# A spectral mixer with an MLP on one core: when the gates' row is multiplied in, and in which order w1's and w2's rows are loaded

## The chip, the cores and the metric

The kernel runs on one core of one Trainium2 chip. The metric is the device time of one execution in microseconds (us). Seven resources of the core matter here: PE (TensorE, the matmuls), DVE (VectorE), ACT (ScalarE), POOL (GpSimd), SP (SyncE, which only issues DMA transfers), the 16 DMA engines, and PSUM, the banks that matmuls write and that DVE and ACT read. Each engine carries out its own instructions strictly in order and waits at an instruction until the work that it needs has been done.

## The reference

```python
def _A_ref(x, ...):                      # Fourier mixing
    a = einsum("bsd,ed->bse", x, dft_hid_re); b = einsum("bsd,ed->bse", x, dft_hid_im)
    return einsum("ts,bse->bte", dft_seq_re, a) - einsum("ts,bse->bte", dft_seq_im, b)
def _B_ref(x, w1, b1, w2, b2):           # the MLP
    h = gelu(einsum("bsd,df->bsf", layernorm(x), w1) + b1)
    return einsum("bsf,fd->bsd", h, w2) + b2
x = A_x                                  # 1 x 2048 x 1024
sa, ca, ga, sb, cb, gb = six rows of silu(c) @ w_mod
x = x + ga * _A_ref(layernorm(x) * (1 + ca) + sa, ...)
x = x + gb * _B_ref(layernorm(x) * (1 + cb) + sb, w1, b1, w2, b2)
```

The inner size of the MLP is 3584, all numbers are float32. `gb` is the row of gates: 1024 numbers, one per column, the same for each of the 2048 tokens.

## The kernel before

**Number format.** The float32 operands are split into a high and a low part in float16, and each product takes three passes (high x high, high x low, low x high). ACT makes the high part (L2379), DVE the low part (L2391). The big products follow Strassen's idea: 7 products of half-size blocks instead of 8, in the order 0, 1, 2, 4, 3, 6, 5. The sums of blocks that this needs are called combs here; DVE adds them (L2405). All data lies in one tensor of the on-chip memory, so nearly every tile has the name `arena`; `ps` is PSUM, `fw` are split weights that were stored in DRAM and are loaded again.

**Stages.** First the two Fourier products and the residual. Then, for 16 tiles of 128 tokens in 8 blocks b0 to b7, the second layer norm: sums (L3138, L3139), squares on ACT (L3120), a root (L2620 on ACT, L2626 on DVE, twice per block), scalings (L3158, L3162 on DVE, L3171 on ACT), a store of the residual to the output (L3148, on SP's queue), eight transposes on PE (L3181: "turn" 0 to 15, one for each tile; 12 and 13 belong to b6, 14 and 15 to b7), copies out of PSUM (L3185), and the split of the result into parts that go to DRAM (L3211, L3220, L3233, stores L3226). Beside it PE computes the six rows of `w_mod` (L2900; loads L2894, a copy out of PSUM by ACT L2923; DVE multiplies `b2` by the gates at L2928, POOL stores the rows at L2924 and L2929).

Then the MLP: `gemm3(g)`, g = 0 to 27, computes the first product (L3628, 7 products of 12 matmuls), each g for 128 columns of w1 and their partners, and `gemm4(v)`, v = 0 to 13, the second (L3742, 2 token blocks of 7 products of 12 matmuls). A half of the tokens is done at v = 0 to 6, the other at v = 7 to 13. The first two g are interleaved (`gemm3_first`): their first products are products 1, 2, 3, 4 and so on in the text, and products 1 to 3 start at 312.04, 318.23 and 322.07 us, product 4 at 341.75. For these, ACT copies a PSUM bank out (L3928), DVE adds the next product to it (L3933) and ACT takes the gelu (L3924); later g use L3650, L3654 and L3647. Results of `gemm4` go to eight running sums `acc`: ACT writes the first ones (L3782), DVE adds all others (L3792). Some products of `gemm4` add onto a bank that already holds another product, and so can start only when that one has been read.

**The loads of weights.** w1 is split once for each g below 14, w2 once for each v below 7. For the first g the split parts were stored early and are loaded again (L3480 for g 0 and 1, L3487 for g 2). Raw rows of w1 for g 3 and 4 are loaded at L3491 (four loads of 256 KB), and at L3494 four loads of 512 KB bring rows of w2 whose sum of squares sets the scale `s2c` of w2's split for v = 0 (L3311 on ACT squares them, L3319 on DVE and L3323 on POOL add them up). The rows for the split itself come at L3497.

**What sets the order.** The program is written by a list planner that runs when the kernel is built. Work is pushed as tasks in streams, each with an engine, a cost, the tasks that it depends on and a due time. The planner keeps a modelled clock for each engine and, whenever PE's next product is placed, puts in front of it those tasks of the other engines that can run by then, those with the earlier due time first. A load is a task of SP's queue in the same way. So a due time doesn't delay anything on the chip: it changes the order in which instructions stand on each engine, and through the modelled clocks that of all that follow.

**The gates.** After `gemm4(5)` and `gemm4(12)`, the last but one of each half, `gb_tasks` multiplies the eight sums `acc` by the row of gates (L3830, 128 x 1024 each); the last `gemm4` of the half then adds its products scaled by the same row. In the second half four further additions (L3835) bring in rows of the output that were stored before (loads L3823), since the last stores don't add.

## Time and profile before

| | |
|---|---|
| time, median of 3 runs | 1378.37 us (1377.45 to 1378.69) |
| profiled execution | 1377.23 us, span 1375.4 us |
| mean granted clock of PE | 0.972 |
| PE busy | 1291.3 us, 94% of the span, 6081 matmuls |
| DVE busy | 1088.4 us, 79% |
| ACT busy | 746.6 us, 54% |
| POOL busy | 265.1 us, 19% |
| L3628, first product | 2352 matmuls, 515.5 us |
| L3742, second product | 2352 matmuls, 513.2 us |
| HBM traffic | 222 GB/s over the span |

The span is that of the profiled execution from its first instruction to its last. The profile's rows name an engine, a line of the kernel, an operation and its tiles (output, arrow, inputs), how many instructions a row joins, and in square brackets the idle time just ahead of it on that engine and what ended it. A row of the timeline begins with its start and its duration in us. "SPq" is an instruction of SP's that issues a DMA transfer; such rows show when it was issued, not when the data had landed.

### The profile page before, as it was taken

What the parts mean: (1) busy time and instruction counts of PE and PEld (TensorE: products, weight loads), DVE (VectorE), ACT (ScalarE), POOL (GpSimd) and SP (SyncE); (2) the same over time, 40 slices, a digit from 0 to 9 for tenths busy, and PEclk for the clock granted to TensorE, in tenths of its full rate; (3) what the DMA queues carried; (4) which work ended last, traced back from release to release, by engine and by line L of the source; (5) the groups of instructions that cost most, each with busy time, mean ns of one, the idle gap of its engine ahead of it and who ended that gap; (6) DMA issues with size and microseconds to landing.
All of it is one profiled execution on the core that took longest, in us unless ns stands there. A gap on an engine that the chain in (4) does not pass through costs nothing.

```text
span 1375.4 us, 17329 instructions
## 1 busy us (share of the span) xinstructions
PE 1291.3 (94%) x6081; PEld 622.9 (45%) x6081; DVE 1088.4 (79%) x1623; ACT 746.6 (54%) x1188; POOL 265.1 (19%) x426
## 2 busy tenths in 40 slices
PE   5888899777989999999999999999999999999997
PEld 1445466543434444444444444444444444444443
DVE  5888789998588999898989996566685858687695
ACT  4476557877667747474746433256545353636330
POOL 2000010102102000000000000254553433553201
PEclk9888899998999999999999999999999999999999
DMA  9777046569536957575453555999797878786524
GB/s 368 307 250 231 1 169 169 133 194 381 218 145 200 320 146 226 171 204 187 153 184 130 200 205 223 262 349 338 252 318 240 296 264 294 268 306 235 176 81 111
DMA packets 109754, 306.22 MB, mean 223 GB/s; under 512 B 14076, under 2 KB 14076, under 8 KB 107736
## 3 DMA queue, kind: packets, MB, share of 16 engines
q1 hardware_dynamic: 76776, 197.73, 40.5%
q0 software_dynamic: 32880, 107.29, 25.9%
q8 instruction: 49, 0.80, 0.2%
q14 instruction: 49, 0.40, 0.1%
HBM read 220.03 MB, written 84.93 MB: 222 GB/s over the span
## 4 chain that ended last, share of the span: by engine, by line
PE 67%; DVE 9%; ACT 4%; issue 2%; DMA 2%; SPq 0%; POOL 0%; DVEq 0%; ACTq 0%; POOLq 0%
PE ps L3742 34%; PE ps L3628 32%; ACT arena L2379 1%; DVE arena L2391 1%; DVE arena L3220 1%; DVE arena L2405 1%; DVE arena L3162 1%; PE ps L3046 1%; DVE arena L3233 1%; DMA arena<-fw 1%; DMA fzc<-arena 1%; ACT arena L3211 1%; DVE arena L3792 0%; DMA arena<-in_w_dram 0%; PE ps L3058 0%
## 5 line engine op out<-in xcount | busy, mean ns | idle before, releaser
L3628 PE MATMUL ps<-arena 128*128 128x512 f16 x2352 | 515.5, 381 | 9.4 <-DMA arena<-fw 4.8
L3742 PE MATMUL ps<-arena 128*128 128x512 f16 x2352 | 513.2, 380 | 8.0 <-ACT arena L3782 6.2
L3628 PEld LDWEIGHTS <-arena 128*128 128x128 f16 x2352 | 230.8, 98 | 289.9 <-issue 10.8
L3742 PEld LDWEIGHTS <-arena 128*128 128x128 f16 x2352 | 230.7, 98 | 288.3 <-issue 12.0
L3792 DVE SCALAR_TENSOR_TENSOR arena<-ps,i4c,arena 128x1024 f32<-128x1024 f32 x179 | 229.5, 1282 | 104.9 <-PE ps L3742 100.4
L2379 ACT ACTIVATE arena<-arena,shc 128x512 f16<-128x512 f32 (+1 forms) x115 | 115.8, 1017 | 137.2 <-DVE arena L2405 80.3
L2391 DVE SCALAR_TENSOR_TENSOR arena<-arena,shc 128x512 f16<-128x512 f32 (+1 forms) x115 | 129.0, 1121 | 29.6 <-ACT arena L2379 29.2
L2405 DVE TENSOR_TENSOR arena<-arena 128x512 f32<-128x512 f32 (+1 forms) x196 | 148.5, 764 | 3.7
L3533 ACT ACTIVATE arena<-arena 128x512 f32<-128x512 f32 (+5 forms) x148 | 91.2, 617 | 108.8 <-DVE arena L3542 84.8
L3647 ACT ACTIVATE arena<-arena,b1s,i1c 128x512 f32<-128x512 f32 x78 | 63.4, 813 | 90.0 <-DVE arena L3654 88.1
L2379 ACT ACTIVATE arena<-arena,s1c 128x512 f16<-128x512 f32 (+1 forms) x70 | 60.9, 886 | 66.5 <-DVE arena L2405 42.2
L3654 DVE TENSOR_TENSOR arena<-arena,ps 128x512 f32<-128x512 f32 x78 | 53.4, 685 | 52.4 <-PE ps L3628 51.7
L3542 DVE TENSOR_TENSOR arena<-arena 128x256 f32<-128x256 f32 x240 | 87.9, 421 | 1.7 <-DMA arena<-in_cre_dram 1.7
L3323 POOL PARTITION_ALL_REDUCE sums<-sums x21 | 10.4, 501 | 405.0 <-DVE sums L3319 405.0
L3559 POOL DMA_DIRECT2D arena<-in_cim_dram x99 | 54.5, 551 | 92.3 <-ACT arena L3533 86.1
L2391 DVE SCALAR_TENSOR_TENSOR arena<-arena,s1c 128x512 f16<-128x512 f32 (+1 forms) x70 | 65.8, 958 | 5.0 <-ACT arena L2379 4.9
L3559 POOL DMA_DIRECT2D arena<-in_cre_dram x99 | 54.6, 552 | 68.3 <-ACT arena L3533 50.9
L3650 ACT ACTIVATE arena<-ps 128x512 f32<-128x512 f32 x78 | 45.8, 588 | 35.8 <-PE ps L3628 35.6
L2391 DVE SCALAR_TENSOR_TENSOR arena<-arena,s2c 128x1024 f16<-128x1024 f32 x49 | 62.0, 1279 | 0.9 <-ACT arena L2379 0.9
L3046 PE MATMUL ps<-arena 128*128 128x256 f16 (+3 forms) x400 | 51.7, 290 | 10.1 <-DVE arena L3073 10.1
L2900 PE MATMUL ps<-arena,scol 128*128 128x512 f32 x128 | 58.3, 602 | 0.3 <-ACT arena L2915 0.3
L2379 ACT ACTIVATE arena<-arena,s2c 128x1024 f16<-128x1024 f32 x49 | 55.0, 1137 | 5.8 <-DVE arena L2405 5.8
(204 smaller groups left out, 1230.7 us busy)
## 6 DMA issues: line engine op xcount, KB each, us to landing
fw<-arena SPq DMA_DIRECT2D x71, 512.0 KB, 5.0
arena<-fw SPq DMA_DIRECT2D x119, 256.0 KB, 4.9
arena<-fw SPq DMA_DIRECT2D x49, 512.0 KB, 7.0
arena<-in_cre_dram POOLq DMA_DIRECT2D x96, 256.0 KB
arena<-in_cim_dram POOLq DMA_DIRECT2D x96, 256.0 KB
arena<-in_wm_dram SPq DMA_DIRECT2D x32, 512.0 KB, 7.5
arena<-in_w_dram SPq DMA_DIRECT2D x32, 512.0 KB, 6.4
arena<-in_w_dram SPq DMA_DIRECT2D x56, 256.0 KB, 4.5
```

The source lines that it names most:

```text
L2379: act.activation(o[m][0], q(j), AF.Copy, **sc)
L2391: dve.scalar_tensor_tensor(o[m][1], q(j), scale, o[m][0], op0=ALU.mult, op1=ALU.subtract)
L2405: dve.tensor_tensor(q(d), q(a), q(b), op=op)
L2900: pe.matmul(bank((6 if n < 3 else 4) + h), scol[:, k : k + 1].to_broadcast([P, P]), FA(o + 512 * h, (1, 512)), start=k == 0, stop=k == 7,)
L3046: pe.matmul(PA(pb + o, (1, w)), l, r, start=n == 0, stop=n == len(mm_) - 1)
L3533: f = lambda: act.activation(sq(a), sq(a), AF.Square, accum_out=csum[0:pn, n : n + 1])
L3542: dve.tensor_tensor(a[:, o::2], a[:, o::2], b[:, o::2], op=op)
L3559: return lambda t: gp.dma_start(t[0:pn], v)
L3628: pe.matmul(ps.rearrange("p (k t) -> p k t", k=4), w1c[:, m, s, a, d * P : (d + 1) * P], zc(m)[:, b, :, d, :], start=(start and d == 0 and ...
L3647: act.activation(dst, src, AF.Gelu_apprx_tanh, scale=inv, bias=b1s[:, 2 * p + j : 2 * p + j + 1])
L3742: pe.matmul(t[:, j], hidc[:, c_, m, a, k * P : (k + 1) * P], w2c[:, m, c_, w], start=(start and c_ == 0 and n == 0), stop=(c_ == 1 and n = ...
L3792: lambda: dve.scalar_tensor_tensor(dst, ps[b], inv, dst, op0=ALU.mult, op1=ALU.add), kp[b],
```

## The change

Two edits. First, the four loads at L3494 (w2's rows for the squares of v = 0) get the due time 300 in place of 240; the four loads of w1's rows just above have 250. Second, the eight multiplications by the gates are pushed in two lots of four: those of token block 0 already within `gemm4(5)` and `gemm4(12)`, at the third product of token block 1, each now depending on the last product of its own block; those of block 1 after `gemm4` as before, with the four additions.

```diff
     for q in range(4):
         f = lambda q=q: sp.dma_start(early2(q), w2[0:2, :, q, :].rearrange("j p x -> p j x"))
-        load(("early2", q), f, [("P", 15), ("Q", 15)], 1.5, "rw3", 240.0)
+        load(("early2", q), f, [("P", 15), ("Q", 15)], 1.5, "rw3", 300.0)
...
-    def gb_tasks(h):
+    def gb_tasks(h, blk):
+
 
         t = []
-        for i in range(8):
+        for i in range(4 * blk, 4 * blk + 4):
             f = lambda i=i: dve.tensor_tensor(acc_tile(i), acc_tile(i), gb2_t, op=ALU.mult)
-            t.append(Task("dve", 1.23, f))
-        if h:
+            t.append(Task("dve", 1.23, f, [("acc", blk, 5)]))
+        if h and blk:
             for m, (r, hf) in LASTQ.items():
...
             if v == NV - 1 or blk == 0:
                 return
+            if v in (5, 12) and slot == 2:
+                push("gb", "gb", gb_tasks(v // 7, 0), due[4, v + 1] - 25.0)
...
             if v in (5, 12):
-                push("gb", "gb", gb_tasks(v // 7), due[4, v + 1] - 25.0)
+                push("gb", "gb", gb_tasks(v // 7, 1), due[4, v + 1] - 25.0)
```

No instruction of PE, DVE or ACT is added or removed by these edits, but the planner's order changes between about 300 and 640 us on every engine but PE, and at the two places of the multiplications. On PE only transposes move. Three places matter below; names and lines of a row are those above, with three lines more from `gb_tasks` on (old L3830 is L3831, L3835 is L3836, L3924 is L3927, L3928 is L3931, L3933 is L3936).

The first is SP's queue from the loads of w2 on, around 300 to 330 us. Before:

```order
L3494 DMA arena_65<-in_w_dram 128x2x512 x3
L3491 DMA arena_65<-in_w_dram 128x512 x2
L3148 DMA out_dram<-arena_65 128x1024
L3491 DMA arena_65<-in_w_dram 128x512 x2
L3487 DMA arena_65<-fw_2_78 128x1024
L3480 DMA arena_65<-fw_0_76 128x1024
L2894 DMA arena_65<-in_wm_dram 128x1024 x5
L3480 DMA arena_65<-fw_1_77 128x1024
L3148 DMA out_dram<-arena_65 128x1024
L2926 DMA arena_65<-in_b_dram 128x1024
```

After:

```order
L3491 DMA arena_65<-in_w_dram 128x512 x2
L3494 DMA arena_65<-in_w_dram 128x2x512 x3
L3148 DMA out_dram<-arena_65 128x1024
L3494 DMA arena_65<-in_w_dram 128x2x512
L3487 DMA arena_65<-fw_2_78 128x1024
L3148 DMA out_dram<-arena_65 128x1024
L3480 DMA arena_65<-fw_0_76 128x1024
L2894 DMA arena_65<-in_wm_dram 128x1024 x5
L3480 DMA arena_65<-fw_1_77 128x1024
L3480 DMA arena_65<-fw_0_76 128x1024
L3480 DMA arena_65<-fw_1_77 128x1024
L2926 DMA arena_65<-in_b_dram 128x1024
```

The second store L3148 (b7's first tile) has moved from behind the first reloads L3480 and the five loads of `w_mod` to ahead of them, and two reloads more stand ahead of the load of `b2` (L2926).

The second is ACT around 335 to 350 us, where the last block b7 (`lns_22`) is normalised. Before:

```order
L2923 ACTIVATE arena_65<-ps 128x1024
L3185 ACTIVATE arena_65<-ps 128x1024
L3211 ACTIVATE arena_65<-arena_65 128x2x512
L3120 ACTIVATE arena_65,lns_22_142<-arena_65,lns_22_142 128x1024
L3185 ACTIVATE arena_65<-ps 128x1024
L3120 ACTIVATE arena_65,lns_22_142<-arena_65,lns_22_142 128x1024
L3928 ACTIVATE arena_65<-ps 128x512
L2620 ACTIVATE lns_22_142<-lns_22_142,eps_13_114 128x2
```

After:

```order
L3120 ACTIVATE arena_65,lns_22_142<-arena_65,lns_22_142 128x1024 x2
L3311 ACTIVATE arena_65,sums_2282<-arena_65 128x1024
L3211 ACTIVATE arena_65<-arena_65 128x2x512
L3311 ACTIVATE arena_65,sums_2282<-arena_65 128x1024
L3211 ACTIVATE arena_65<-arena_65 128x512
L2923 ACTIVATE arena_65<-ps 128x1024
L3185 ACTIVATE arena_65<-ps 128x1024
L2620 ACTIVATE lns_22_142<-lns_22_142,eps_13_114 128x2
L2621 ACTIVATE lns_22_142<-lns_22_142,eps_13_114 128x2
L3931 ACTIVATE arena_65<-ps 128x512
```

The root L2620 of b7 stood behind the copy of product 4 (L3928) and now stands ahead of it (L3931); its squares L3120 stand ahead of L2923.

The third is DVE around 1328 to 1345 us, between `gemm4(12)` and `gemm4(13)`. Before:

```order
L3830 TENSOR_TENSOR arena_65<-arena_65 128x1024
L2405 TENSOR_TENSOR arena_65<-arena_65 128x512 x2
L3792 SCALAR_TENSOR_TENSOR arena_65<-ps,i4c_152,arena_65 128x2x512
L3835 TENSOR_TENSOR arena_65<-arena_65 128x2x512
L3792 SCALAR_TENSOR_TENSOR arena_65<-ps,i4c_152,arena_65 128x2x512
L2405 TENSOR_TENSOR arena_65<-arena_65 128x512
L2391 SCALAR_TENSOR_TENSOR arena_65<-arena_65,shc_149 128x512
L3835 TENSOR_TENSOR arena_65<-arena_65 128x2x512 x2
```

After:

```order
L2391 SCALAR_TENSOR_TENSOR arena_65<-arena_65,shc_149 128x512 x2
L2405 TENSOR_TENSOR arena_65<-arena_65 128x512 x3
L3792 SCALAR_TENSOR_TENSOR arena_65<-ps,i4c_152,arena_65 128x2x512
L2391 SCALAR_TENSOR_TENSOR arena_65<-arena_65,shc_149 128x512 x2
L3792 SCALAR_TENSOR_TENSOR arena_65<-ps,i4c_152,arena_65 128x2x512
L2391 SCALAR_TENSOR_TENSOR arena_65<-arena_65,shc_149 128x512
L2405 TENSOR_TENSOR arena_65<-arena_65 128x512
L3836 TENSOR_TENSOR arena_65<-arena_65 128x2x512 x2
```

No multiplication stands any more directly ahead of the combs L2405 of the last g, and the additions (L3835, now L3836) stand behind them.

## The prediction

> **What bounds the kernel now.** I read the page first, then what PE (TensorE) waits for, PE's timeline, the two 20-us windows in which it is slow, and last the rows of the engines that it waits for there.
>
> ```profile
> PE 1291.3 (94%) x6081; PEld 622.9 (45%) x6081; DVE 1088.4 (79%) x1623; ACT 746.6 (54%) x1188; POOL 265.1 (19%) x426
> ```
>
> ```profile
> PE ps L3742 <- ACT arena L3782: 6.2, 1, 6.2
> PE ps L3628 <- DMA arena<-fw: 4.8, 2, 3.7
> PE ps L3628 <- DVE arena L3073: 3.3, 1, 3.3
> PE ps L3742 <- DVE arena L3792: 1.4, 2, 1.2
> PE ps L3628 <- ACT arena L3650: 1.3, 2, 0.7
> PE ps L3742 <- DVE arena L2391: 0.4, 1, 0.4
> ```
>
> The first line is the page's: PE is busy in 94% of the span, and its number of matmuls doesn't change. The six others are every wait of the MLP's products (L3628 first, L3742 second product; columns: us in total, times, longest). PE's timeline says where they lie:
>
> ```profile
> 312.04 5.28 PE L3628 MATMUL ps<-arena 128*128 128x512 f16 x12 [3.29 <-DVE arena L3073]
> ...
> 322.07 2.76 PE L3628 MATMUL ps<-arena 128*128 128x512 f16 x12 [1.09 <-DMA arena<-fw]
> ...
> 341.75 17.25 PE L3628 MATMUL ps<-arena 128*128 128x512 f16 x72 [3.73 <-DMA arena<-fw]
> ...
> 368.54 1.09 PE L3181 MATMUL ps<-ident,arena 128*128 128x128 f32 x8 [0.90 <-ACT arena L3185]
> 369.47 23.65 PE L3628 MATMUL ps<-arena 128*128 128x512 f16 x108
> 392.95 5.34 PE L3742 MATMUL ps<-arena 128*128 128x512 f16 x24
> 404.50 33.82 PE L3742 MATMUL ps<-arena 128*128 128x512 f16 x144 [6.21 <-ACT arena L3782]
> ...
> 476.21 4.05 PE L3742 MATMUL ps<-arena 128*128 128x512 f16 x18
> ...
> 1339.71 1.04 PE L3742 MATMUL ps<-arena 128*128 128x512 f16 x4 [0.43 <-DVE arena L2391]
> ...
> 1344.89 22.18 PE L3742 MATMUL ps<-arena 128*128 128x512 f16 x102 [1.25 <-DVE arena L3792]
> ```
>
> So the waits lie in two places: the hand-over from the transforms to the MLP (312 to 476 us) and 1339 to 1345 us. Between 476 and 1339 the products never wait. What PE gains or loses before 476 therefore reaches the end unchanged, and DVE work moved between those times is worth nothing unless it makes PE wait. The early multiplications at v=5 (about 800 us) lie there: I cost them at nothing; their cover is PE's unbroken work.
>
> A matmul costs 23.65/108 = 0.219 us at full clock. After the wait of 6.21 the 144 took 33.82 instead of 144 x 0.219 = 31.5: 2.3 us for a lower clock. After the wait of 3.73 the 72 took 1.5 more than 15.8. In the windows of 20 us that hold the waits of 3.29 and 6.21 (the last three columns are the granted clock, the DMA share and GB/s) the granted clock is 0.83, so the loss is the clock's:
>
> ```profile
> 310.00:330.00 20.00, 16.48 (x61) 7.72 (x61) 16.74 (x32) 16.66 (x28) 4.20 (x7) 0.83 1.02 397
> 390.00:410.00 20.00, 13.79 (x53) 5.62 (x52) 18.68 (x19) 11.73 (x14) 1.41 (x2) 0.83 0.50 191
> ```
>
> The Trainium skill (TensorE: Matmul & The Clock Gate, "What's actually happening") says that after an idle window of about 3.4 us the array runs at half clock until it has been busy for about as long. By that the penalty would be about 1.7 us, an estimate from the page; the sum would then come out 0.6 us smaller. The row's 2.3 decides here.
>
> **The loads.** The change puts 4 loads of 512 KB of w2 behind w1's 4 of 256 KB. The bytes are the same, and in both orders all eight stand ahead of the reload (L3480) that product 3 waits for, so this alone moves nothing. What matters is what the planner then did: on SP the store L3148 of b7's first tile (b7 is the last token block) now stands ahead of that reload (old issue 317.78) instead of behind it.
>
> ```profile
> 317.78 0.38 SPq L3480 DMA_DIRECT2D arena<-fw  x1
> ...
> 328.49 0.34 SPq L3148 DMA_DIRECT2D out_dram<-arena  x1
> ...
> 332.44 4.29 SPq L3480 DMA_DIRECT2D arena<-fw  x4
> ```
>
> ```profile
> SPq L3148 <- DVE arena L3139: 6.5, 1, 6.5
> ```
>
> ```profile
> fw<-arena SPq DMA_DIRECT2D x71, 512.0 KB, 5.0
> arena<-fw SPq DMA_DIRECT2D x119, 256.0 KB, 4.9
> ```
>
> In the old order that store blocked SP for 6.5 us, because its sum L3139 came late on DVE. In the new order L3139 follows its first half L3138 at once, both ahead of the L3158 pair:
>
> ```profile
> 313.64 2.48 DVE L3158 SCALAR_TENSOR_TENSOR arena<-arena,lns 128x1024 f32<-128x1024 f32 x2
> 316.03 1.22 DVE L3138 TENSOR_TENSOR arena<-arena 128x1024 f32<-128x1024 f32 x1
> ...
> 327.24 1.22 DVE L3139 SCALAR_TENSOR_TENSOR arena<-arena 128x1024 f32<-128x1024 f32 x1
> ...
> 348.74 0.69 DVE L3933 TENSOR_TENSOR arena<-arena,ps 128x512 f32<-128x512 f32 x1 [6.29 <-PE ps L3628]
> ```
>
> So it ends at 313.64 + 2 x 1.22 = 316.1, and SP, which reaches the store at 317.8, hardly waits. Product 3's reload has one more transfer of 512 KB ahead, 1.3 us at the window's 397 GB/s, and one issue (0.34): **product 3 +1.7**, at 323.8, ending at 326.6. Bounds: 0 (hidden among transfers in flight) and +12 (the store stays at 328.49: the second rival).
>
> Product 3's copy on ACT now stands ahead of b6's second squares (L3120):
>
> ```profile
> 323.48 1.13 ACT L3120 ACTIVATE arena<-arena,lns 128x1024 f32<-128x1024 f32 x1
> ...
> 334.93 1.02 ACT L2923 ACTIVATE arena<-ps 128x1024 f32<-128x1024 f32 x1 [0.95 <-PE ps L2900]
> ...
> 346.08 0.60 ACT L3928 ACTIVATE arena<-ps 128x512 f32<-128x512 f32 x1 [4.95 <-PE ps L3628]
> 346.58 0.29 ACT L2620 ACTIVATE lns<-lns,eps 128x2 f32<-128x2 f32 x1
> ...
> 356.94 1.23 ACT L3171 ACTIVATE arena<-arena,lns 128x1024 f32<-128x1024 f32 x1
> ```
>
> They start at 326.6 + 0.6 = 327.2 instead of 323.48, so turn 12, the w_mod rows L2900 behind it and L2923 come **3.7 later** (L2923 at 338.6). Product 4's reload (old issue 332.44) takes a buffer that those L2900 rows free, and stands behind the store of b7's second tile, whose L3139 comes on DVE after b6's root: 327.2 + two squares 2.3 + roots and small ones 1.4 + 0.7 + 2 x 1.22 = 334.0. With two loads between it is issued near 336.0. The old one took 9.3 us to product 4's start, behind five w_mod loads; these are now 1.7 later and this one 3.5, so I take the mean of the page, 4.9: **product 4 at 340.9** (old 341.75). The ends are 4.9 and 9.3, so up to 345.3.
>
> **The last token block.** b7's root L2620 no longer stands behind product 4's copy, which waited 4.95 us for PE. It comes after L2923 and one more copy of the same length: 338.6 + 2 x 1.02 = 340.6, **6.0 us earlier**. From the old root to L3171 were 10.4 us, of which 2.3 went by on DVE behind L3933 (348.74) and 1.6 on ACT behind a copy. L3171 comes between 340.6 + 6.5 = 347.1 and 351.0, instead of 356.94. PE reaches turn 14 after 12 matmuls, turn 13 and 36 matmuls: 340.9 + 48 x 0.219 + 1.1 = 352.5, so nothing waits there. After 48 more comes turn 15 at 364.0 (old 368.54), after 120 more the second product: 364.0 + 1.0 + 26.3 = 391.3, against 392.95: **-1.6**. (12 matmuls more than before stand behind turn 15, which takes 2.6 of the 4.5 back.) One step is later: the row store of the gates (L2929) has its multiplication L2928 behind an add of product 6 now, near 351; with 5.0 for a store it lands at 357, and the copy that waits for it is asked for by PE at 353.5 + 24 x 0.219 = 358.8. Hidden by 1.2; bounds 0 and +2.
>
> **The wait of 6.21.** The third product of gemm4(0) adds onto a bank that ACT must have read:
>
> ```profile
> 400.23 3.23 ACT L2379 ACTIVATE arena<-arena,s2c 128x1024 f16<-128x1024 f32 x3 [3.10 <-DVE arena L2405]
> 403.36 1.09 ACT L3782 ACTIVATE arena<-ps,i4c 128x1024 f32<-128x1024 f32 x1
> ```
>
> The read (L3782) stands behind splits of w2, and these behind combs on DVE. In the new order two of five splits stand earlier, and splits of w1 (L2391) behind. Between DVE's last add of the first pair and the last comb I count 10 L2391 (8 x 1.28, 2 half as wide x 0.64), 9 L2405 (4 x 1.22, 5 x 0.71) and 3 L3654 (0.68), by the rows below: 22 us. The add follows the first 12 matmuls behind turn 15: 365.0 + 2.6 + 0.7 = 368.3. The last comb ends at 390.3, with 2 us for waits on ACT at 392.3; two splits of 1.08 and L3782 end at 395.6. PE asks at 391.3 + 5.3 = 396.6. **-6.2**, and with it the lower clock **-2.3**. Bounds: all stays (0) or all goes (-8.5); I take all, and each us over the margin of 1.0 would cost one.
>
> **The next hand-over, gemm4(1).** What is late next: five of the seven low splits of w2 (L2391) and two combs now stand behind the last add of the g before, all ahead of the first L3792. In the old order one did.
>
> ```profile
> 464.10 1.22 DVE L2405 TENSOR_TENSOR arena<-arena 128x1024 f32<-128x1024 f32 x1
> ...
> 474.02 0.68 DVE L3654 TENSOR_TENSOR arena<-arena,ps 128x512 f32<-128x512 f32 x1
> 474.62 1.28 DVE L2391 SCALAR_TENSOR_TENSOR arena<-arena,s2c 128x1024 f16<-128x1024 f32 x1
> ```
>
> The add ends 1.5 us before PE starts gemm4(1) (474.70, 476.21). Then 5 x 1.28 + 2 x 1.22 + 1.28 for L3792 = 10.1, so the eviction is in 8.6 us after PE's start; the third product asks at 5.3: **+3.3**. Bounds: 0 (the splits run earlier than their place) and +5.6 (with a clock penalty of 2.3).
>
> **The end.** At v=12 two of the sixteen multiplications go between evictions of the same round, and hid27's combs (L2405) stand directly ahead of gemm4(13)'s first L3792, the kept adds behind:
>
> ```profile
> 1330.52 1.41 DVE L2405 TENSOR_TENSOR arena<-arena 128x512 f32<-128x512 f32 x2
> ```
>
> The waits of PE at 1339 to 1345 (0.43, 1.25 and the 0.15 that makes the row's 1.4) end on DVE. With two multiplications (2.4 us) and two adds out of the way they go: **-1.8**; bounds 0 and -1.8. On SP the four loads of kept rows now follow w2's seven loads; their adds stand later too, beside PE's last 102 matmuls (22.18 us), so I cost that at nothing; if they came later than that, the end would move.
>
> **Sum.** -1.6 - 6.2 - 2.3 + 3.3 - 1.8 = -8.6 us. The profiled execution took 1377.23 us (span 1375.4), 1.1 below the runs' median of 1378.37; the sum goes to the median: **1369.8**, or -0.6%. Covered work: w2's scale comes later with its squares (L3311 on ACT), but they stand ahead of L2923 (338.6), and their first user, the split of w2 (L2379), stands behind turn 15's copies.
>
> **Rivals.**
> 1. The third product still waits. DVE is busy 18.68 of 20 us in the window 390 to 410; if its work, not the transposes, sets the end of this stage, the 8.5 stay, and with them the old lead of DVE at gemm4(1), so the 3.3 falls away: -1.6 - 1.8, 1375.0.
> 2. Slower: the store L3148 on SP waits until its old 328.49. Product 3's reload, five w_mod loads and product 4's reload stand behind it, and PE idles 12 us more. As the forecast has PE without a wait from 340.9 on, each us late there reaches the end: -8.6 + 12 = +3.4, with 2.3 more for the clock, 1381.8 to 1384.1. It decides from 8.6 us late. For it: that store did wait 6.5. Against: L3138 ran at 316.03 with no wait.
> 3. The stage doesn't change in sum (b6's 3.7 late and product 4's slower reload eat b7's gain); only the end does: 1376.6.
>
> **Chances.** Forecast 0.55, rival 1 0.13, rival 3 0.10, rival 2 and anything slower 0.17, better than 1363 0.05. The forecast's own range is 1364 (without the 3.3 and with the 0.9 and 1.3 of old waits gone too: -14.1) to 1374 (product 4 at 345.3: +4.4). The range that takes in rivals 1 and 3 is 1363 to 1379. A difference under 0.2% (2.8 us) can't be told from none: forecast, better and half of rival 1 make faster 0.68 (half of rival 1 is 0.07, rounded up), the rest of it and rival 3 same 0.15, slower 0.17.
>
> **What will show it.** Right: SP's wait on L3139 ahead of product 3 gone, b7's root near 341, turn 14 near 352 and turn 15 near 364 without a wait, the row of 144 matmuls starting near 397 at about 31.5 us, gemm4(1) starting 8 to 11 us before 476 with a wait of some 3 us at its third product, and the rows of 1339 to 1345 gone. Wrong: an SP wait ahead of product 3 that stays, product 4 later than 346, a wait of L3742 on L3782 that stays, or new waits of PE between 476 and 1339.

## The result, and the profile after

| | before | after |
|---|---|---|
| median of the runs side by side | 1377.45 us (1375.72 to 1378.69) | 1371.72 us (1370.14 to 1374.18) |
| ratio | | 0.9964, 95% interval 0.9947 to 0.9981 |
| profiled execution | 1377.23 us, span 1375.4 | 1370.87 us, span 1368.9 |
| mean granted clock | 0.972 | 0.974 |

The changed kernel is 5.7 us (0.4%) faster; 8.6 us were forecast. The profiled executions differ by 6.5 us in the span, and the rows up to the experiments are read from these two. PE's timeline of the changed kernel, in the same place as the one shown for before:

```profile
324.24 4.45 PE L3628 MATMUL ps<-arena 128*128 128x512 f16 x12 [3.34 <-DMA arena<-fw]
...
343.78 2.76 PE L3628 MATMUL ps<-arena 128*128 128x512 f16 x12 [1.53 <-DMA arena<-fw]
...
355.41 1.09 PE L3181 MATMUL ps<-ident,arena 128*128 128x128 f32 x8 [0.21 <-ACT arena L3171]
356.34 5.34 PE L3628 MATMUL ps<-arena 128*128 128x512 f16 x24
363.61 5.34 PE L3628 MATMUL ps<-arena 128*128 128x512 f16 x24 [1.93 <-ACT arena L3931]
368.78 1.04 PE L3181 MATMUL ps<-ident,arena 128*128 128x128 f32 x8
...
395.56 5.34 PE L3742 MATMUL ps<-arena 128*128 128x512 f16 x24
401.18 31.24 PE L3742 MATMUL ps<-arena 128*128 128x512 f16 x144 [0.29 <-ACT arena L3782]
432.26 36.42 PE L3628 MATMUL ps<-arena 128*128 128x512 f16 x168
468.52 5.34 PE L3742 MATMUL ps<-arena 128*128 128x512 f16 x24
476.62 31.25 PE L3742 MATMUL ps<-arena 128*128 128x512 f16 x144 [2.75 <-DVE arena L3792]
507.71 12.46 PE L3628 MATMUL ps<-arena 128*128 128x512 f16 x57
...
1305.42 18.29 PE L3628 MATMUL ps<-arena 128*128 128x512 f16 x84
...
1335.74 24.77 PE L3742 MATMUL ps<-arena 128*128 128x512 f16 x114 [0.37 <-DVE arena L3792]
```

The reader is to see four things. The wait of 6.21 us is now 0.29, and the 144 matmuls behind it take 31.24 us instead of 33.82. Yet gemm4(0) starts at 395.56, later than before (392.95). A wait of 2.75 has come to gemm4(1). And of the waits that before has between 1339 and 1345 us one of 0.37 is left (at 1335.74 here).

For the bookkeeping, PE's rows of before that the prediction did not need, from the end of gemm4(0) to the end of gemm4(1):

```profile
438.16 5.34 PE L3628 MATMUL ps<-arena 128*128 128x512 f16 x24
...
476.21 36.42 PE L3742 MATMUL ps<-arena 128*128 128x512 f16 x168
512.47 0.81 PE L3628 MATMUL ps<-arena 128*128 128x512 f16 x3
```

The forecast's sum against the two timelines (after less before, us):

| term | forecast | measured | from |
|---|---|---|---|
| start of gemm4(0) | -1.6 | +2.6 | 395.56 - 392.95 |
| wait of its third product | -6.2 | -5.9 | 0.29 - 6.21 |
| clock behind it | -2.3 | -2.6 | 31.24 - 33.82 |
| g behind it: the two waits on L3650 (1.3) and 0.5 around them, at full clock (1.00) | none | -1.8 | 438.16 to 476.21 is 38.05, 432.26 to 468.52 is 36.26 |
| gemm4(1) | +3.3 | +2.9 | 468.52 to 507.71 is 39.19, 476.21 to 512.47 is 36.26 |
| end | -1.8 | -1.8 | from the start of the row of 84 L3628 to the end of the last L3742: 55.09, before 56.88 |
| sum | -8.6 | -6.6 | span -6.5 |

Between the first product behind gemm4(1) and the row of 84 L3628 the changed kernel takes 797.71 us (1305.42 - 507.71) and before 797.72 (1310.19, where that row starts in its timeline, - 512.47). So the multiplications at v = 5 moved nothing that PE shows, as forecast.

One correction to the description of the kernel: products 1 to 7 are all of g 0 and those of g 1 follow, so product 3 is the third of g 0. No step of the prediction rested on it.

### Where the start of gemm4(0) was lost

The one term with the wrong sign begins at product 3. SP's queue (issues), then what SP waited for between 305 and 322 us and between 330 and 340 us:

```profile
317.13 0.34 SPq L3487 DMA_DIRECT2D arena<-fw  x1
317.56 0.38 SPq L3148 DMA_DIRECT2D out_dram<-arena  x1
318.03 0.38 SPq L3480 DMA_DIRECT2D arena<-fw  x1
...
336.12 0.34 SPq L3148 DMA_DIRECT2D out_dram<-arena  x1
...
337.87 1.29 SPq L3480 DMA_DIRECT2D arena<-fw  x2
```

```profile
SPq L3487 <- PE ps L3628: 5.6, 1, 5.6
```

```profile
SPq L3148 <- DVE lns L3150: 5.5, 1, 5.5
```

From 305 to 322 us SP also waited 5.2 us for DVE's L3139; that is for the store before, issued at 310.52, which waited 5.9 us for DVE in the kernel before too. The store of b7's first tile (317.56) issues right behind L3487, which waited for product 1 to end; DVE's sum had ended at 315.9 and didn't hold it. So the second rival's mechanism did not come: the reload was issued at 318.03, only 0.25 us after before's 317.78. But its data arrived later: from issue to product 3 it was 6.2 us, before 4.3. That is the +1.7 that was forecast for one more transfer of 512 KB, with 0.2 on top. What the forecast left out is that PE's wait there grew from 1.09 to 3.34 us, and that product 3 then ran at a low clock: 4.45 us instead of 2.76 (granted clock 0.60 from 324.3 to 328.6 us, in before 1.00 from 322.1 to 324.8).

The delay passes on. ACT, DVE and POOL of the changed kernel:

```profile
329.22 1.14 ACT L3120 ACTIVATE arena<-arena,lns 128x1024 f32<-128x1024 f32 x1
...
344.11 0.30 ACT L2620 ACTIVATE lns<-lns,eps 128x2 f32<-128x2 f32 x1
...
362.96 0.60 ACT L3931 ACTIVATE arena<-ps 128x512 f32<-128x512 f32 x1 [2.51 <-DMA frow_gbb<-arena]
...
396.92 3.21 ACT L2379 ACTIVATE arena<-arena,s2c 128x1024 f16<-128x1024 f32 x3
400.04 1.09 ACT L3782 ACTIVATE arena<-ps,i4c 128x1024 f32<-128x1024 f32 x1
```

```profile
346.01 0.15 DVE L3327 TENSOR_SCALAR sums<-sums 128x1 f32<-128x1 f32 x1 [1.84 <-POOL sums L3323]
...
346.91 0.16 DVE L2626 RECIPROCAL lns<-lns 128x2 f32<-128x2 f32 x1
...
354.59 1.22 DVE L2928 TENSOR_TENSOR arena<-arena 128x1024 f32<-128x1024 f32 x1
...
471.69 3.67 DVE L2391 SCALAR_TENSOR_TENSOR arena<-arena,s2c 128x1024 f16<-128x1024 f32 x3
475.28 2.66 DVE L3792 SCALAR_TENSOR_TENSOR arena<-ps,i4c,arena 128x1024 f32<-128x1024 f32 x2
```

```profile
356.11 0.56 POOL L2929 DMA_DIRECT2D frow_gbb<-arena  x1 [2.85 <-DVE arena L2928]
```

b6's second squares start at 329.22 (forecast 327.2), the store of b7's second tile is issued at 336.12 (its sum was forecast for 334.0), product 4's reload at 337.87 (336.0) and product 4 at 343.78 (340.9). Then the row of gates: L2928 runs at 354.59 (near 351), its store L2929 lands when ACT goes on at 362.96, 6.9 us after its issue, and PE waits 1.93 us at 363.61. On DVE the scale of w2 (L3327 and what follows) waits 1.84 us for POOL and stands ahead of b7's root (L2626), which had been ready since 344.4.

The last two rows of ACT show why the wait of 6.21 is gone: ahead of the three splits of w2 and L3782 ACT had stood idle for 3.10 us before, for a comb of DVE's, and now it starts them at 396.92 without a wait.

### The profile page after: what moved, and what is told of

It is laid out like the page before. It is cut to its first block, busy times and chain, and to the rows that moved or that the text cites. A ratio compares the mean times of both kernels' runs of the same rounds, so it can differ in the third digit from the quotient of the medians.

```text
span 1368.9 us, 17332 instructions
## 1 busy us (share of the span) xinstructions
PE 1290.3 (94%) x6081; PEld 623.7 (46%) x6081; DVE 1089.1 (80%) x1623; ACT 747.7 (55%) x1188; POOL 263.8 (19%) x426
## 4 chain that ended last, share of the span: by engine, by line
PE 67%; DVE 10%; DMA 2%; ACT 2%; issue 2%; SPq 1%; POOL 0%; DVEq 0%; POOLq 0%; ACTq 0%
PE ps L3742 34%; PE ps L3628 32%; DVE arena L2391 2%; DVE arena L3220 1%; DVE arena L3162 1%; DVE arena L2405 1%; DVE arena L3233 1%; ACT arena L2379 1%; PE ps L3046 1%; DMA arena<-in_wm_dram 1%; DMA fw<-arena 1%; DMA frow_gbb<-arena 0%; DVE arena L3158 0%; DMA arena<-fw 0%; DVE arena L3073 0%
## 5 line engine op out<-in xcount | busy, mean ns | idle before, releaser
L3628 PE MATMUL ps<-arena 128*128 128x512 f16 x2352 | 515.3, 381 | 9.8 <-DMA arena<-fw 4.9
L3742 PE MATMUL ps<-arena 128*128 128x512 f16 x2352 | 510.4, 379 | 3.4 <-DVE arena L3792 3.1
L3628 PEld LDWEIGHTS <-arena 128*128 128x128 f16 x2352 | 230.7, 98 | 290.5 <-issue 10.4
L3742 PEld LDWEIGHTS <-arena 128*128 128x128 f16 x2352 | 229.9, 98 | 281.6 <-DVE arena L3792 3.2
L3792 DVE SCALAR_TENSOR_TENSOR arena<-ps,i4c,arena 128x1024 f32<-128x1024 f32 x179 | 229.4, 1282 | 104.3 <-PE ps L3742 102.4
L2405 DVE TENSOR_TENSOR arena<-arena 128x512 f32<-128x512 f32 (+1 forms) x196 | 148.8, 764 | 4.0 <-ACT arena L3647 0.3
L3650 ACT ACTIVATE arena<-ps 128x512 f32<-128x512 f32 x78 | 45.9, 589 | 34.9 <-PE ps L3628 34.8
L2900 PE MATMUL ps<-arena,scol 128*128 128x512 f32 x128 | 59.6, 613 | 0.3 <-ACT arena L2915 0.3
L3311 ACT ACTIVATE ps<-arena 128x1024 f32<-128x1024 f32 x46 | 46.7, 1016 | 18.7 <-DMA arena<-in_w_dram 9.1
```

What stands on the lines that cost most here:

```text
L2405: dve.tensor_tensor(q(d), q(a), q(b), op=op)
L2900: pe.matmul(bank((6 if n < 3 else 4) + h), scol[:, k : k + 1].to_broadcast([P, P]), FA(o + 512 * h, (1, 512)), start=k == 0, stop=k == 7,)
L3628: pe.matmul(ps.rearrange("p (k t) -> p k t", k=4), w1c[:, m, s, a, d * P : (d + 1) * P], zc(m)[:, b, :, d, :], start=(start and d == 0 and ...
L3742: pe.matmul(t[:, j], hidc[:, c_, m, a, k * P : (k + 1) * P], w2c[:, m, c_, w], start=(start and c_ == 0 and n == 0), stop=(c_ == 1 and n = ...
L3792: lambda: dve.scalar_tensor_tensor(dst, ps[b], inv, dst, op0=ALU.mult, op1=ALU.add), kp[b],
```

## The experiments

Each was run beside before on one chip. A mark is a difference of two starts in the trace of one execution: the *hand-over* is from product 1 to the first product behind gemm4(1) (200.43 us in before: 512.47 - 312.04; 195.89 after: 507.71 - 311.82), *to turn 15* is from product 1 to that row of transposes, and the *end* as above. Product 1's own start lay between 307 and 313 us, so marks tell more than the span of one execution. But a mark also holds what the clock did in that one execution: the 12 matmuls of product 1 took 5.28 us in most of these traces, 4.72 with the loads swapped back, and 4.12 to 4.24 in both of the gates alone and in the kernel with three edits. Lines of an experiment's rows can be up to 10 higher than those of the changed kernel.

| kernel | ratio to before, 95% interval | to turn 15 | hand-over | end |
|---|---|---|---|---|
| before | | 56.50 | 200.43 | 56.88 |
| after | 0.9964 (0.9947 to 0.9981) | 56.96 | 195.89 | 55.09 |
| after, again | 0.9952 (0.9935 to 0.9970) | 56.53 | 195.44 | 55.08 |
| due time only | 0.9982 (0.9970 to 0.9995) | 56.22 | 195.32 | 56.89 |
| due time only, again | 0.9979 (0.9967 to 0.9991) | 57.22 | 197.83 | 56.88 |
| gates only | 0.9996 (0.9982 to 1.0010) | 56.76 | 202.28 | 55.08 |
| gates only, again | 0.9978 (0.9966 to 0.9990) | 56.52 | 200.89 | 55.08 |
| loads swapped back | 0.9956 (0.9941 to 0.9971) | 55.56 | 196.18 | 55.09 |
| scale of w2 later | 0.9961 (0.9948 to 0.9974) | 54.89 | 195.35 | 55.09 |
| splits of gemm4(1) earlier | 0.9997 (0.9984 to 1.0011) | 57.25 | 201.93 | 55.09 |
| store behind the reload | 0.9942 (0.9924 to 0.9961) | 53.86 | 194.47 | 55.09 |
| eviction ahead of two splits | 0.9954 (0.9938 to 0.9970) | 58.98 | 195.52 | 55.09 |
| scale later, store behind, eviction first: all three | 0.9919 (0.9898 to 0.9941) | 52.34 | 188.73 | 55.08 |
| all three, and the reload first | 0.9907 (0.9887 to 0.9927) | 51.00 | 187.38 | 55.09 |

### The two edits apart

```diff
-        load(("early2", q), f, [("P", 15), ("Q", 15)], 1.5, "rw3", 240.0)
+        load(("early2", q), f, [("P", 15), ("Q", 15)], 1.5, "rw3", 300.0)
```

alone is the first kernel; the second edit (`gb_tasks` in two lots) alone is the other.

> Only the due time of w2's four loads is changed (240 to 300); the eight multiplications stay together after gemm4(5) and gemm4(12). Theory (two independent places): PE's products run past 507 us as in the changed kernel, 4.8 us ahead of the kernel before, with the 6.21 us wait on L3782 gone and some 2.8 us of wait at gemm4(1); the waits at the end (0.43, 0.15, 1.25) stay. Together -4.8 us, a ratio of 0.9965. Rival (the waits at the end went because the stage before them came earlier): -6.3 us, 0.9954. Rival (the gain comes from the multiplications): no change.

> Only the eight multiplications are split into two lots of four; w2's loads keep due 240. Theory: nothing changes up to 1290 us, the three waits at 1339 to 1345 shrink from 1.83 to about 0.4: -1.5 us, a ratio of 0.9989. Rival (only the due time counts): 0 us. Rival (moving the multiplications at v = 5 matters too): a difference that shows on PE before 850 us.

Measured: the due time alone shows the hand-over of the whole change (195.32) and before's end (56.89); the gates alone show about before's hand-over (202.28, 1.9 more) and the new end (55.08). In the traces the two parts lie apart. The times of the runs are less so: the due time alone gives 0.9982 and the gates alone 0.9996, together less than the whole change's 0.9964. Both were run again, with the changed kernel beside them.

> The changed kernel once more, beside the others of this call on one chip. Its median was 5.7 us below before's, while the trace of it shows 6.5 less in the span and 5.6 less from product 1 to the first product behind gemm4(1) and 1.8 at the end. Product 1's own start scattered from 307 to 313 us between kernels with the same order up to there. If the marks of the trace are the change and the start is chance, the ratio comes out at 0.993 to 0.997 again, with product 1 to the first product behind gemm4(1) at 195 to 197 us and the end at 55.1. If the start belongs to the change, the start is again above 311 and the ratio near 0.996.

> The loads' due time alone, once more: its trace gave 5.1 us less than before from product 1 to the first product behind gemm4(1) and nothing at the end, its runs only 2.5 us less (interval 0.7 to 4.1). By the trace: a ratio of 0.996 to 0.9975 here, above the whole change by 0.0013, the 1.8 us of the end. By the runs: 0.998 again, and the gain of the due time is then smaller than the one trace says, and what is left over comes from somewhere that this trace doesn't show.

> The gates' two lots alone, once more: the trace gave 1.8 us less at the end and nothing or 1 to 2 more in the hand-over, the runs 0.5 less (from 2.5 less to 1.4 more). By the end alone the ratio is 0.9987; if the two lots also cost something in the hand-over, 0.9995 to 1.0005. Together with the due time alone it should give the ratio of the whole change, if the two edits don't touch each other.

PE's rows in the second run of the gates alone, and gemm4(1) in the second run of the due time alone:

```profile
390.29 5.34 PE L3742 MATMUL ps<-arena 128*128 128x512 f16 x24
401.84 34.15 PE L3742 MATMUL ps<-arena 128*128 128x512 f16 x144 [6.20 <-ACT arena L3782]
```

```profile
477.08 32.94 PE L3742 MATMUL ps<-arena 128*128 128x512 f16 x144 [2.75 <-DVE arena L3792]
```

Without the due time the wait of 6.2 us and its low clock stay, so they are the due time's doing. The changed kernel came out at 0.9952 with product 1 at 307.72, where it had been at 311.82: the late start did not belong to the change. The gates alone gave 0.9978; the 1.8 us of the end make 0.9987 of before's 1375, and both of their intervals hold that. Which part of that edit does it, the multiplications or the additions that moved with them, is not separated. The due time alone again gave less than its first trace says: -5.1 would be 0.9963, which neither of its intervals holds. Its second trace shows a hand-over of 197.83, that is -2.6 or 0.9981, which both hold: 1.7 us of the difference between its two traces are the clock in the row above (32.94, in its first trace 31.25 behind a wait of 2.94). So a part of the due time's gain is there in some executions and not in others; how often is not known from two traces, and stays open.

### The order of the loads by itself

The changed kernel's plan, with nothing but the eight raw loads given out in before's order:

```diff
+    f8 = {"r": [], "e": []}
+    def next8():
+        k = "e" if f8["e"] else "r"
+        f8[k].pop(0)()
...
-        load(("early2", q), f, [("P", 15), ("Q", 15)], 1.5, "rw3", 300.0)
+        f8["e"].append(lambda q=q: sp.dma_start(early2(q), w2[0:2, :, q, :].rearrange("j p x -> p j x")))
+        load(("early2", q), next8, [("P", 15), ("Q", 15)], 1.5, "rw3", 300.0)
```

> The changed kernel with every engine's order kept, except that on SP the eight raw loads stand in the old order again: w2's four for the squares first, then w1's four. It separates the order of the bytes from what the planner made of it. Theory (the order of these loads alone moves nothing, the gain is the re-planned order): as the changed kernel, within 0.5 us from the first product to gemm4(2), 0.9955 to the kernel before by the traces. Rival (the loads themselves are the gain, since w1's rows or the reload of product 3 land earlier behind them): the stage falls back by up to 4.5 us, 0.9985.

Measured: 0.9956, hand-over 196.18, and gemm4(0)'s third product waits as in the changed kernel:

```profile
324.16 4.20 PE L3635 MATMUL ps<-arena 128*128 128x512 f16 x12 [3.14 <-DMA arena<-fw]
...
400.81 31.24 PE L3749 MATMUL ps<-arena 128*128 128x512 f16 x144 [0.29 <-ACT arena L3789]
```

The nearness of the two hand-overs, 0.3 us, is partly chance: to turn 15 this trace is 1.4 us shorter, 0.9 of it ahead of product 2, and the 144 matmuls of gemm4(1) ran at a low clock (32.94 us, 31.25 in the changed kernel). But the fall of up to 4.5 us that the rival asks for is not there, and the wait of 6.2 us doesn't come back. So w2's rows behind w1's are worth nothing that these runs show. What the due time does, it does through the order that the planner gives the other work from there on.

### The scale of w2, and the row of gates

```diff
-    push("w2n", "n2_0", w2_norm(0), 240.0)
+    push("w2n", "n2_0", w2_norm(0), 270.0)
```

on top of the change. The planner then sets the scale of w2 behind b7's root on DVE, and L2928 and L2929 earlier.

> The changed kernel, with the due time of the squares and the scale of w2 for v = 0 put from 240 to 270. On DVE the scale's six small operations, which wait for POOL, then stand behind b7's second root instead of ahead of its first, and the multiplication L2928 stands 20 rows earlier, so that its store lands before ACT's copy needs it. What the delay of b7's root (346.9 instead of 344.6 us) was worth is in question. Theory: PE waited only 0.21 us for it at turn 14, so it is worth 0.2, and the copy's wait for the store 1.93: together about -2.1 us against the changed kernel, a ratio of 0.9949 to the kernel before. Rival (the root sets the pace): -2.3 - 1.9 = -4.2 us, 0.9933. Rival (the later scale makes w2's splits late): the wait on L3782 comes back, no gain.

```profile
342.87 1.22 DVE L2928 TENSOR_TENSOR arena<-arena 128x1024 f32<-128x1024 f32 x1
...
352.67 0.15 DVE L3327 TENSOR_SCALAR sums<-sums 128x1 f32<-128x1 f32 x1
```

```profile
353.87 10.52 PE L3628 MATMUL ps<-arena 128*128 128x512 f16 x48
...
391.27 36.66 PE L3742 MATMUL ps<-arena 128*128 128x512 f16 x168
```

Measured: the wait on the gates' row is gone (48 matmuls in one row, where the changed kernel has 24 and 24 with 1.93 between), turn 15 is 2.1 us nearer to product 1, and the third product of gemm4(0) shows no wait any more. Of these 2.1 the wait was 1.9; b7's root, though it no longer waits for the scale, gave nothing that PE could use, since turn 14 had waited only 0.21. The hand-over shows 0.5 and not 2.1, because gemm4(1)'s 144 matmuls fell to the low clock this time (32.94 us). The time, 0.9961, can't be told from the changed kernel's.

### gemm4(1): its splits

Two attempts on the new wait of 2.75 us. The first pushes all of w2's splits for v = 1 earlier:

```diff
-        push("w2", f"w2_{v}", w2_tasks(v) if v < 7 else w2_loads(v), due[4, v])
+        push("w2", f"w2_{v}", w2_tasks(v) if v < 7 else w2_loads(v), due[4, v] - (15.0 if v == 1 else 0.0))
```

> The changed kernel, with w2's split tasks for v = 1 due 15 us earlier, so that on DVE six of the seven low splits stand ahead of the last add of the g before instead of two. Theory: the wait of 2.75 us at gemm4(1)'s third product goes and nothing takes its place: -2.75 us against the changed kernel, 0.9944 to the kernel before. Rival (DVE has no room there: it is busy 19 of 20 us at 450 to 470 in the kernel before): what is pushed back, the splits of the hidden layer and of w1, makes PE wait later by as much: 0 us.

```profile
466.40 4.28 PE L3742 MATMUL ps<-arena 128*128 128x512 f16 x19 [0.92 <-DVE arena L2391]
476.08 33.27 PE L3742 MATMUL ps<-arena 128*128 128x512 f16 x144 [5.41 <-DVE arena L3792]
```

A miss of the theory, and worse than the rival: the wait doubled, and the hand-over is 6 us longer than in the changed kernel. In this trace DVE stands idle for only 1.4 us between the last add of the g before (462.23) and the first eviction (474.75), and what fills that time is mostly splits of the hidden layer and of w1 and their combs: what was put earlier pushed them behind the add.

The second leaves the time of the splits and puts the two last ones, which only later products need, behind the first eviction L3792:

```diff
+        elif v == 1:
+            need(f"hid{2 * v}", f"hid{2 * v + 1}")
+            for m in (0, 1, 2, 4):
+                emitted(("w2", v, m))
...
+                if v == 1:
+                    emitted(("w2", v, m))
...
+                        slack=-9.0 if (v, blk, m) == (1, 0, 0) else 0.6,
```

> The changed kernel with one move on DVE at gemm4(1): its first eviction L3792 stands ahead of the last two splits of w2 instead of behind them (the order of some splits after it shifts with that). Theory (the third product waited for DVE's queue, not for its work in all): 2 x 1.28 us of splits less ahead, so the wait of 2.75 falls to 0.3: -2.4 us against the changed kernel. Rival (DVE is full, so the splits behind come late for their own products): the wait goes to a later product of gemm4(1), gain 0.

```profile
468.96 1.28 DVE L2391 SCALAR_TENSOR_TENSOR arena<-arena,s2c 128x1024 f16<-128x1024 f32 x1
470.16 2.67 DVE L3798 SCALAR_TENSOR_TENSOR arena<-ps,i4c,arena 128x1024 f32<-128x1024 f32 x2
```

```profile
359.19 7.03 PE L3628 MATMUL ps<-arena 128*128 128x512 f16 x24 [2.08 <-ACT arena L3938]
...
471.50 31.25 PE L3746 MATMUL ps<-arena 128*128 128x512 f16 x144 [0.36 <-DVE arena L3798]
```

Measured: gemm4(1) takes 36.8 us (465.79 to 502.59) instead of 39.2, with 0.36 left of the wait. So the term of the forecast was what it was said to be: splits ahead of the first eviction on DVE. In this trace the clock took 1.7 us back elsewhere: the 24 matmuls behind the gates' row took 7.03 us instead of 5.34. The time, 0.9954, can't be told from the changed kernel's.

### The store ahead of the reload

On top of the change, the store L3148 of b7's first tile is issued right behind product 3's reload:

```diff
-            store("x1", i, lambda n=n, i=i: sp.dma_start(o_s[i // 8, i % 8], y[:, n]), k)
+            f = lambda n=n, i=i: sp.dma_start(o_s[i // 8, i % 8], y[:, n])
+            store("x1", i, (lambda f=f: late.append(f)) if i == 14 else f, k)
...
+                if (g, m) == (0, 2):
+                    late.pop(0)()
```

> The changed kernel with two neighbours on SP swapped: the store L3148 of b7's first tile behind the reload that product 3 waits for, as in the kernel before. Theory (the prediction's +1.7 for the store ahead, and the clock that falls after the longer wait): product 3 waits 1.1 instead of 3.34 us and runs in 2.76 instead of 4.45, L2900 and all that follows 3.8 us earlier, and it reaches the end: -3.8 us against the changed kernel. Rival (the wait is only shifted: product 4's reload or the gates' store L2929, which ACT waited for, take it up): product 3 is earlier, but turn 15 by less than 1.5 us.

```profile
318.84 2.76 PE L3632 MATMUL ps<-arena 128*128 128x512 f16 x12 [0.93 <-DMA arena<-fw]
323.17 3.70 PE L2900 MATMUL ps<-arena,scol 128*128 128x512 f32 x8 [1.57 <-DMA arena<-in_wm_dram]
...
337.91 4.45 PE L3632 MATMUL ps<-arena 128*128 128x512 f16 x12 [4.43 <-DMA arena<-fw]
```

Measured: product 3 starts 9.97 us behind product 1 (318.84 - 308.87) instead of 12.42, waits 0.93, and runs at full clock. That is about before's wait (1.09), and it shows the first link of the chain: the store ahead of the reload cost the longer wait and, with it, the clock. Product 4 comes 29.0 us behind product 1 instead of 32.0; but it waits 4.43 for its own reload and now runs at the low clock itself, and with a wait of 0.35 on the gates' row in place of 1.93 turn 15 is 3.1 us nearer to product 1. So a part of the wait was shifted, as the rival has it, but more than its 1.5 us was won. The hand-over is only 1.4 us shorter, because gemm4(1)'s 144 matmuls ran at a low clock (32.94 us). The time is 0.9942; its interval overlaps with the changed kernel's.

### All three, and one step more

The scale of w2 later, the store behind the reload and the eviction first, together:

> The changed kernel with the scale of w2 put later (as in e3), the store behind the reload (as in e6) and the eviction first (as in e7). Theory (three places, each on PE's path): -2.1 - 3.8 - 2.4 = -8.3 us against the changed kernel, 0.990 to the kernel before. Rival (DVE then sets the pace of the stage): the wait of gemm4(0)'s third product on L3782 comes back and gives some 3 us of it back.

```profile
312.28 4.24 PE L3632 MATMUL ps<-arena 128*128 128x512 f16 x12 [2.47 <-DVE arena L3073]
...
322.11 4.45 PE L3632 MATMUL ps<-arena 128*128 128x512 f16 x12 [2.13 <-DMA arena<-fw]
```

Measured: 0.9919 (0.9898 to 0.9941), hand-over 188.73, 7.2 less than the changed kernel; the 168 matmuls of gemm4(0) run in one row (36.66 us) and gemm4(1) has 0.37 left. Of the 7.2, 1.4 belong to this execution and not to the edits: product 1 took 4.24 us here, and product 2 came that much sooner. Product 3 waited 2.13 us and ran at the low clock. That too is partly this execution's: the reload was there 9.83 us behind product 1, as with the store behind it alone (9.97), but PE stood ready 1.4 us sooner. The next step takes the wait for one of SP's order and puts the load L3487 of w1's first row for g 2 behind that reload too:

```diff
-            sp.dma_start(w1c[:, m, 0], w1_d[2][:, m])
+            g = lambda: sp.dma_start(w1c[:, m, 0], w1_d[2][:, m])
+            late.append(g) if m == 0 else g()
...
-                    late.pop(0)()
+                    while late:
+                        late.pop(0)()
```

> The three edits of the last kernel together (the scale of w2 later, the store L3148 behind product 3's reload, the last two splits of w2 for gemm4(1) behind its first eviction), and one step more: the load L3487 of w1's first row for g 2 goes behind that reload too. Theory (on SP's queue each DMA ahead of a reload delays it by its own issue and its share of the transfers): in the kernel with the three edits product 3 still waited 2.13 us and ran at the low clock (4.45 for its first 12 matmuls against 2.75). With nothing but w2's rows ahead, that wait goes to 0 to 1 and the 1.7 with it: 2 to 4 us less than that kernel, from product 1 to turn 15 some 49 us, a ratio to the kernel before of 0.988 to 0.991. Rival (the reload waits for transfers that are in flight already, and not for its place): the same time as with three edits, about 0.992, product 3 waiting about 2 us, or the wait moves to product 4 behind it, 52 us from product 1 to turn 15.

SP's and PE's rows of this kernel, and the window around the reload (the last three columns are granted clock, DMA share, GB/s):

```profile
311.35 0.48 SPq L3482 DMA_DIRECT2D arena<-fw  x1
...
316.96 0.34 SPq L3492 DMA_DIRECT2D arena<-fw  x1
```

```profile
321.54 2.76 PE L3634 MATMUL ps<-arena 128*128 128x512 f16 x12 [0.75 <-DMA arena<-fw]
...
339.35 2.76 PE L3634 MATMUL ps<-arena 128*128 128x512 f16 x12 [3.17 <-DMA arena<-fw]
```

```profile
312.00:320.00 8.00, 8.00 (x30) 3.90 (x29) 6.73 (x9) 4.64 (x9) 2.43 (x4) 0.65 1.04 410
```

Measured: 0.9907 (0.9887 to 0.9927), the fastest of all: 1362.48 us, where before took 1375.35 and the changed kernel 1369.53 beside it. The time is the theory's, the mechanism mostly the rival's. The reload is issued 5.6 us earlier than L3487 and 0.3 us ahead of product 1, and still product 3 starts 9.89 us behind product 1. With the store behind the reload alone it was 9.97, though the reload was issued only 5.75 us behind product 1 (314.62); there 4.2 us went by from issue to product, here 10.2. The DMA engines are full in this window (share 1.04, 410 GB/s). What was won over the kernel with three edits is the 1.7 us of the low clock at product 3, which didn't come in this trace: product 1 took 5.28 us again, so PE came later and waited 0.75. Product 4's wait grew from 1.17 to 3.17 us. To turn 15 are 51.0 us and not 49. That this kernel beats the one with three edits isn't shown: their intervals overlap. That it beats the changed kernel is: 0.9927 at most against 0.9935 at least.

## Why the prediction was right, and where it was wrong

**Right in direction, 1.9 us low in the median** (1369.8 against 1371.72), inside its range; as a difference to before, 5.7 us of the 8.6. It went by the sum's mechanism, not by a rival's, but that the sum is only some 2 us off is partly luck: the start of gemm4(0) came 4.2 us worse than forecast, and two waits that the sum left out gave 1.8 back.

**The wait of 6.21.** Right: 0.29 is left and the lower clock is gone (-5.9 and -2.6 against -6.2 and -2.3). The working put ACT's L3782 1.0 us ahead of PE's need. It ended at 401.13, 0.3 behind PE: both came later than forecast, since both hang on turn 15. DVE took what was forecast, 23.6 us from its last add of the first pair to the last comb (24 in the working), but three splits of w2 and not two stood directly ahead of L3782 on ACT, and that used up the margin. That it is the re-planned order and not the loads is shown by the loads swapped back; which of the moved splits did it is not separated.

**The start of gemm4(0): the step that failed.** Forecast -1.6, measured +2.6. Three terms in it were mis-sized. *Product 3 +1.7* was right as far as the transfer goes (the start came at 324.24, forecast 323.8), but it was summed without the clock: behind the wait of 3.34 us PE lost 1.7 more. Keeping the store behind the reload took both away. *Product 4 at 340.9* came at 343.78: 1.9 of it is the chain from product 3 through b6's squares, DVE's sum and the store, and 1.0 is the reload's 5.9 us from issue to product instead of 4.9. (The profile's 4.9 is a median, where the prediction calls it a mean.) *The gates' row, hidden by 1.2*, cost its upper bound, 1.93: L2928 stood 3.6 us later than assumed, and its store of 512 KB took 6.9 us until ACT went on, not 5.0. With L2928 earlier the wait went.

**Covered work: w2's scale.** Wrong in the text: its squares were early enough, but its small operations on DVE stand ahead of b7's root and wait for POOL's sum. It cost little of itself (turn 14 waited 0.21).

**b7's root** came at 344.11, 3.5 later than forecast and 2.5 earlier than before; turn 14 itself came 2.9 later than forecast and so waited only 0.21 for it. The forecast root followed L2923 at 338.6; it came at 342.29, when both its PE rows and ACT's work ahead of it had just ended. On PE the clock had struck a second time: turn 12 and the row of L2900 behind it took 1.62 and 6.52 us instead of before's 1.09 and 5.32 (granted clock 0.78 from 334.3 to 342 us). Of this at most turn 14's 0.21 reached gemm4(0), since product 4 waited 1.53 us for its reload anyway.

**gemm4(1), +3.3.** Right in place and nearly in size (2.9; the wait 2.75), and shown by putting two splits behind the eviction. The clock penalty, held possible there by a bound of 2.3, came in four traces with this wait (1.7 each) and not in three others.

**Two waits on L3650** were not in the sum: 1.8 us more won than forecast. The prediction had their 1.3 only in the lower end of its range.

**The end, -1.8, and v = 5 at nothing:** both right to 0.1 us in the traces, the end with some luck: the sum was to come from three waits (1.83) that go, but one of 0.37 is left, so 0.3 of the 1.8 lies in no wait that the rows show.

**The rivals.** The third product still waiting: no. The store held until 328.49: no, SP issued it at 317.56, and L3487's wait on PE had covered DVE's sum. Only the end changes: no for the whole change; that is what the gates' lots alone show in their traces. The chances of faster and same, 0.68 and 0.15, add up to 0.67 and 0.16 from their parts.

**The clock.** The prediction set the row's 2.3 us against the 1.7 that it estimated from the Trainium skill (TensorE: Matmul & The Clock Gate, "What's actually happening"). Both have their place in the runs: behind the waits of 6.2 us the 144 matmuls took 2.6 to 2.9 more (33.82 and 34.15 against 31.24), while behind waits of 2 to 4 us the loss, where it came, was mostly 1.69 to 1.70.

## What to carry to other kernels

When a term of a sum makes PE wait longer, add the clock to it: here a wait of 2 to 4 us could cost some 1.7 us more, as much as the transfer that caused it. A due time in a list planner is no local edit: the order of the loads showed no worth of its own, and what the planner made of it decided the whole hand-over, so read the new order on each engine at each wait and not the diff. Once one such wait is gone, look at what else stands ahead of the next ones on the same engine; here three small moves behind the change won about as much again (0.9919 against 0.9952 and 0.9964). And before a few us in one trace are put down to an edit, look whether the clock took or gave them: executions of one kernel differ by such steps.

## What the runs showed of the hardware

The clock's penalty behind short waits is mostly one step. In most traces product 3's 12 matmuls take 2.76 or 4.45 us, and in the rows above 24 take 5.34 or 7.03 and 144 take 31.25 or 32.94: 1.69 to 1.70 apart. The granted clock goes with it: 1.00 in the changed kernel from 476.7 to 483 us, 0.71 in the second run of the due time alone from 477.1 to 483. It is not always that step: product 3 also took 4.20 to 4.34 us in four traces, and behind longer waits the 144 lost more, 2.0 behind 5.41 us and 2.6 to 2.9 behind 6.2. The same wait of 2.75 us at gemm4(1) led to 31.25 us in both runs of the changed kernel and to 32.94 in four others (the scale of w2 later, the store behind the reload, the loads swapped back, the due time alone again). The Trainium skill (TensorE: Matmul & The Clock Gate, "What's actually happening") tells of a free-running window of about 3.4 us; half of that is the step seen here, and that the same wait is charged in one execution and not in the next would fit a window that runs free. But the page asks for an idle window of 3.4 us, and here waits of 2.08 and 2.75 were charged; and behind the wait of 6.21 us the granted clock was 0.52 over the 5.5 us from 404.5 on, longer than one such window. In this the measurement decides, and what the window counts is not shown.

In this stage a reload that was issued earlier did not land earlier. The DMA engines were full (share 1.04, 410 GB/s from 312 to 320 us in the last kernel); issued 0.3 us ahead of product 1 the reload was there 9.89 us behind it, and issued 5.75 us behind product 1, with the store behind the reload, 9.97 us behind it. These are two traces; whether it holds elsewhere is not shown.
